# A long convolution and a cosine-gated layer on one core: the data as stationary operand of the last transform step, blocks of x turned by VectorE, and places of 129 elements

## The chip, the cores and the metric

The kernel runs on one core of a Trainium2 chip. The metric is device time in microseconds (us), from the start of the program to its end; lower is better. A core has a matrix engine (TensorE, PE in the profile; its weight loads are the row PEld), VectorE (DVE), ScalarE (ACT), GpSimd (POOL) and SyncE (SP), which here only issues DMAs. SP issues them in program order on one queue, and 16 DMA engines carry the packets.

## The reference

```python
# x, v (4, 12480, 128); pos_emb (12480, 64); w1 (64, 64); w2 (64, 128)
h = (np.maximum(pos_emb @ w1, 0) @ w2) * np.exp(-0.01 * pos)[:, None]
u = x * v
y = irfft(rfft(u, n=2*S, axis=1) * rfft(h, n=2*S, axis=0), n=2*S, axis=1)[:, :S]
t = (x * y).reshape(49920, 128)
hid = t @ w_in                        # 128 -> 2048
out = (hid * np.cos(hid)) @ w_out     # 2048 -> 128
```

All data are float32. The first part is a causal convolution along the sequence, channel by channel, with a filter h of the sequence's length; the second a layer with a cosine gate ("MoE" in the code's names).

## The kernel before, in words

**The convolution** is a transform of M = 96 x 120 points in two steps each way (N1 = 96, N2 = 120; the sequence is R = 104 rows of 120). One large array in SBUF, `slots`, holds a batch through all steps: per partition 64 pairs of channels, and for each pair 240 places of 2 elements (L807); `parts`, `above` and `aT` are views of it (L808 to L810). A *place* is the set of 128 channels that one index of the transform has in a partition; here its 64 pairs lie 480 elements apart. The steps of a batch:

- *u*: x and v are loaded (`load_pairs`, L373), multiplied (L395) and their sums and differences put into places (L401).
- *f1* (L405): for each of the 128 channels a matmul whose stationary operand ("weights") is the channel's column of `slots` and whose moving operand is a table of 192 columns; evicted (L420) to `parts`.
- *f2* (L442): for each of 48 pairs of indices k1, matmuls with a table `w` (124 partitions) as weights and 256 columns of `slots` moving, then the product with the filter's transform `h` on VectorE and GpSimd (L456). `w` and `h` come from the DRAM tensors `wd` and `hd`. For batch 0 a variant (`f2_both_units`, L610) makes `w` and `h`, uses them and stores them for the later batches.
- *i1* (L477): per channel two matmuls with the channel's column as weights and a table of 120 columns moving; evicted (L484) to places.
- *i2* (L493), the last step: 30 groups g of four indices n2. Each n2 takes two matmuls that add up: the weights are a table `t` (`tm`, 96 x 104), and the moving operand is a place, 128 channels. So a group's result is 104 rows by 4 x 128 channels in a PSUM bank. `i2_out` (L507) multiplies it by x, loaded in the same form as `xs` (L673), and stores it to the DRAM tensor `zd`, one row of 512 elements for each row and group (L517). The tables `tm` are made once in batch 0 (some ahead, L659) and loaded from `td` for the other batches.

While i2 of a batch runs, the loads, products and sums of the next batch run between its groups (`inverse_units`, L688).

**The layer** takes the rows of `zd` in 98 blocks n of up to 128 rows (the first has 104), that is up to 512 tokens of 128 channels, and 16 chunks c of 128 hidden units. `moe_load` (L723) fetches a block as rows (`zb`); `moe_turn` (L730) turns it to channels by tokens with four TensorE transposes (L126 in the profile, a helper's line) and a copy by ScalarE into `at`. A step (n, c) is: the up matmul (L743), ScalarE's scaled copy `a` (L746), VectorE's rounding `k` (L749), GpSimd's difference `f` (L752), ScalarE's sine `cs` (L757), VectorE's product `gt` (L759) and, four steps later (LAG), the down matmul into the accumulator `acc` (L768), which has one PSUM bank (once the convolution is through, every other block takes a bank of its pool). After the last chunk ScalarE copies `acc` to `ot` (L774), `moe_back` (L777) turns it back with four transposes and a copy `ob`, and `moe_store` (L786) stores it with one to three DMAs in runs of 1 KB.

**The order.** Instructions are issued in the order that the program writes them. Every step of the convolution is a generator (`units`, L530, whose parts are `before`: loads, `mm`: matmuls, `after`: evictions, each a `yield` apart). The generators say how many layer steps they are worth; the main loop (L949 to L974) issues one layer step, then as much of the convolution as is owed. So the layer runs beside the convolution of batches 1 to 3 and beside i2 of batch 0, and alone at the end. Until about 338 us the convolution runs alone: the filter, f1 of filter and batch 0, `f2_both` (171 to 270) and i1. `beside` (L876) puts conversions of the layer's weights between units of f1 and i1. i2 of the four batches stands at 338 to 565, 1178 to 1384, 1992 to 2206 and 2815 to 2946 us; the layer alone from about 3000.

All DMAs are issued by SP. Each kind of tile has a few buffers (`bufs`); an instruction that needs a buffer waits until its former user is done.

Of the kernel before, what the change touches and what calls it, by code (L numbers as in the profile page):

```python
# [9 lines left out]
F32 = mybir.dt.float32  # L10
# [20 lines left out]
def kernel(  # L31
# [74 lines left out]
    LAG = 4  # L106
    WCOL = 256

    dram = ctx.enter_context(tc.tile_pool(name="dram", bufs=1, space=DRAM))
    hd = dram.tile([N1 // 2, N2, 2, CB, 4], F32, name="hd")  # L110
    zd = dram.tile([NROWS, G, D], F32, name="zd")
# [241 lines left out]
    def filter_out(pool, bank, aT, slots, j, w2_sb):  # L353
# [5 lines left out]
        above = pool.tile([FR, 2, CB, 2], F32, name="above", bufs=2)  # L359
        pj = ps[0:FR, :].rearrange("p (n b i) -> p n b i", n=4, i=2)  # L360
        nc.scalar.copy(out=above[:, :, :, :], in_=pj[:, 2:4])
        a = H - 2 - 2 * j
        for place, op in ((a, ALU.add), (ODD + a, ALU.subtract)):
            nc.vector.tensor_tensor(
                slots[0:FR, :, place:place + 2, :].transpose([0, 2, 1, 3]),
                pj[:, 1::-1], above[:, :, :, :], op=op)
# [14 lines left out]
    def clear_gap(u):  # L381

        nc.gpsimd.memset(u[:, :, H:ODD, :], 0.0)
# [13 lines left out]
    def u_sums(u, tiles, a):  # L397
        both = tiles[0][:, :, :].rearrange("p h (n b i) -> p h n b i", n=UA, i=2)
        below, above = both[:, 0, ::-1, :, :], both[:, 1, :, :, :]
        for place, op, e in ((a, ALU.add, nc.gpsimd), (ODD + a, ALU.subtract, nc.vector)):  # L400
            e.tensor_tensor(u[0:R, :, place:place + UA, :].transpose([0, 2, 1, 3]),  # L401
                            below, above, op=op)


    def f1_mm(ps, u, b, i):  # L405

        nc.tensor.matmul(ps[0:KE, i * 2 * N1:(i + 1) * 2 * N1], u[:, b, 0:KE, i],  # L407
# [12 lines left out]
    def f1_evict(ps, b, share):  # L420
        copy, negated = f1_takers(b, share)
        pj = ps[:, 0:4 * N1].rearrange("p (i r k) -> p r k i", i=2, r=2)
        copy(out=parts[0:ODD, :, :, b, :], in_=pj[0:ODD])
        yield
        copy(out=parts[ODD:KE, 0, :, b, :], in_=pj[ODD:KE, 1])
        negated(parts[ODD:KE, 1, :, b, :], pj[ODD:KE, 0])
        yield

    def f1_evict_filter(ps, b, share):
# [3 lines left out]
        near, far = ftile[:, b, :, :], above[:, b, :, :]  # L433
# [8 lines left out]
    def f2_mm(ps, w, k1, i, filt=False):  # L442
# [3 lines left out]
        pi = ps[0:N2, :].rearrange("p (r b g i) -> p g r b i", r=2, g=2, i=2)[:, i]  # L446
        if not filt:
            nc.tensor.matmul(pi, w[:, i, :], parts[0:KE, :, k], start=True, stop=True)  # L448
        elif k < KF:
            both = ftile[0:KE, :, k:k + N1 + 1:N1, :].rearrange("p b r i -> p r b i")  # L450
            nc.tensor.matmul(pi, w[:, i, :], both, start=True, stop=True)
        else:
            for r, src in enumerate((ftile[0:KE, :, k, :], above[0:KE, :, k - KF, :])):
                nc.tensor.matmul(pi[:, r], w[:, i, :], src, start=True, stop=True)

    def f2_product(pool, ps, h, k1, whole):  # L456


        y = parts[0:N2, :, k1:k1 + 2, :, :].rearrange("p r k b i -> p r b (k i)")
        t = pool.tile([N2, 2, CB, 4], F32, name="t", bufs=1 + whole)  # L460
        uu = ps[0:N2, :].rearrange("p (r b j) -> p r b j", r=2, j=4)
# [15 lines left out]
    def i1_mm(ps, b, i):  # L477
        for r in range(2):
            nc.tensor.matmul(  # L479
                ps[0:N1, (i * 2 + r) * N2:(i * 2 + r + 1) * N2],  # L480
                parts[0:N2, r, :, b, i],
                cs[:, r, :], start=True, stop=True)

    def i1_evict(pool, ps, b):  # L484
# [3 lines left out]
        for h, op in ((0, ALU.add), (1, ALU.subtract)):  # L488
            nc.vector.tensor_tensor(slots[0:N1, b, h * N2:(h + 1) * N2, :], pj[:, 0],  # L489
                                    other[:, :, :], op=op)  # L490
            yield

    def i2_mm(ps, t, g, part):  # L493
        for i in range(part * G // 2, (part + 1) * G // 2):
# [8 lines left out]
            for r, place in enumerate(places):  # L503
                nc.tensor.matmul(ps[0:R, i * D:(i + 1) * D], t[:, i, r, :],  # L504
                                 slots[0:N1, :, place, :], start=(r == 0), stop=(r == 1))

    def i2_out(pool, ps, xs, b, g):  # L507
        if b == 0:
            yield
        zs = pool.tile([R, 2, UA, D], F32, name="zs")  # L510
        nc.vector.tensor_tensor(
            zs[:, :, :, :].rearrange("p h n d -> p (h n d)"), ps[0:R, :],
            xs[:, :, :].rearrange("p h n -> p (h n)"), op=ALU.mult)
        z = zs[:, :, :, :].rearrange("p h n d -> p (h n) d")
        row = (b * NG + g) * R
        if row > 0:
            nc.sync.dma_start(zd[row:row + R, :, :], z)  # L517
        else:
            zbs[0] = z
        made[0] += 1  # L520
        yield

# [482 lines left out]
```

## Time and profile before

| | before |
|---|---|
| device time, median of 3 runs | 3760.59 us (3759.83 to 3761.09) |
| profiled execution, span | 3758.9 us |
| up matmul L743: records, busy, mean | 3136, 1599.0 us, 591 ns |
| ScalarE copies L737, L774, L783, mean | 574, 574, 584 ns |
| place matmul L504: records, busy, mean | 1920, 251.7 us, 273 ns |
| f2's matmul L448: records, busy, mean | 576, 173.0 us, 380 ns |
| GpSimd's sums L474: records, mean | 384, 821 ns |

The profile is of one execution. A matmul of 512 columns leaves two records, one of 256 columns or fewer leaves one. Matmuls are pipelined, so records overlap and a mean duration is longer than the pace; the pace is read from start to start. "x" behind an engine's time is the count of instructions in a stretch; a wait is written as the waiting instruction, "<-", and what released it, then the total idle time in us, the count and the mean. PEclk is the granted clock of TensorE; it is 1.00 or near it over nearly the whole span.

### The profile page before, as it was taken

Reading aid. Unit: us, or ns where it says so; the run is one execution under the profiler, and the core shown is the slowest. Engines: PE = TensorE matmul, PEld = TensorE weight load, DVE = VectorE, ACT = ScalarE, POOL = GpSimd, SP = SyncE. Lnnn points to the kernel's source line nnn. Section 1 sums busy time; section 2 is a strip of 40 time slices with the busy share of each in tenths; the row PEclk is TensorE's granted clock in tenths of the full one; section 3 lists DMA queues with packets and bytes.
Section 4 is the critical chain, followed back from the end, with each engine's and each line's share of the span. In section 5 each row is a group of like instructions: output and inputs, shape, how many; then the busy total and the mean of one; then the engine's idle time right before and its main releaser. Section 6 shows DMA issues by size and latency. Waiting matters only on the chain.

```text
span 3758.9 us, 47177 instructions
## 1 busy us (share of the span) xinstructions
PE 3690.6 (98%) x13546; PEld 2110.4 (56%) x13546; DVE 2773.7 (74%) x5586; ACT 2508.2 (67%) x4660; POOL 2557.6 (68%) x2318
## 2 busy tenths in 40 slices
PE   7898999999999999999999999999999999999999
PEld 6777555555566556555565556555566544444444
DVE  8887997687866787788766776788765666666666
ACT  5757776766665557766665567666664677777777
POOL 6666776588845665688745664788644677777776
PEclk9999999999999999999999999999999999999999
DMA  6263551022203650122104530122105200000000
GB/s 167 64 185 107 155 167 33 25 72 79 72 12 91 181 151 12 40 79 77 52 18 128 180 105 21 52 79 76 38 21 172 76 23 17 17 23 18 17 23 13
DMA packets 209499, 276.14 MB, mean 73 GB/s; under 512 B 17111, under 2 KB 146535, under 8 KB 209111
## 3 DMA queue, kind: packets, MB, share of 16 engines
q1 hardware_dynamic: 209239, 273.12, 24.8%
q8 instruction: 109, 1.79, 0.2%
q14 instruction: 151, 1.24, 0.1%
HBM read 193.64 MB, written 79.42 MB: 73 GB/s over the span
## 4 chain that ended last, share of the span: by engine, by line
PE 88%; DVE 3%; POOL 3%; ACT 2%; DMA 2%; issue 1%; SPq 0%; POOLq 0%; DVEq 0%; ACTq 0%
PE ph L743 33%; PE acc L768 28%; PE cv L504 5%; PE cv L768 5%; PE cv L479 4%; PE cv L407 3%; PE cv L448 3%; PE ph L126 2%; POOL f L752 1%; PE ps L407 1%; PE ps L448 1%; DMA tm<-td 1%; DMA wd<-w 1%; ACT cs L757 1%; DVE k L749 1%
## 5 line engine op out<-in xcount | busy, mean ns | idle before, releaser
L752 POOL TENSOR_TENSOR f<-a,k 128x512 f32<-128x512 f32 (+1 forms) x1568 | 1986.2, 1267 | 1060.5 <-DVE k L749 1059.1
L743 PE MATMUL ph<-at,w_in_sb 128*128 128x512 f32 (+1 forms) x3136 | 1599.0, 591 | 3.7 <-DVE gt L759 2.7
L746 ACT ACTIVATE a<-ph,quarter 128x512 f32<-128x512 f32 (+1 forms) x1568 | 1071.2, 683 | 704.8 <-PE ph L743 695.2
L768 PE MATMUL acc<-gt,w_out_sb 128*128 128x512 f32 (+1 forms) x2688 | 1370.3, 591 | 0.0
L759 DVE TENSOR_TENSOR gt<-ph,cs 128x512 f32<-128x512 f32 (+1 forms) x1568 | 1077.3, 687 | 359.9 <-ACT cs L757 341.8
L757 ACT ACTIVATE cs<-f 128x512 f32<-128x512 f32 (+1 forms) x1568 | 981.0, 626 | 366.6 <-POOL f L752 364.3
L749 DVE TENSOR_SCALAR k<-a 128x512 f32<-128x512 f32 (+1 forms) x1568 | 792.9, 506 | 550.7 <-ACT a L746 524.2
L768 PEld LDWEIGHTS acc<-gt,w_out_sb 128*128 128x128 f32 x2688 | 508.4, 189 | 642.8 <-issue 631.9
L743 PEld LDWEIGHTS ph<-at,w_in_sb 128*128 128x128 f32 x3136 | 553.2, 190 | 337.7 <-issue 257.5
L474 POOL TENSOR_TENSOR slots<-slots,t 120x256 f32<-120x256 f32 x384 | 312.9, 821 | 59.9 <-DVE t L467 25.6
L504 PEld LDWEIGHTS cv<-slots,tm 96*104 96x104 f32 x1920 | 238.6, 169 | 106.8 <-issue 85.4
L504 PE MATMUL cv<-slots,tm 96*104 96x128 f32 x1920 | 251.7, 273 | 9.9 <-POOL tm L297 5.0
L768 PE MATMUL cv<-gt,w_out_sb 128*128 128x512 f32 (+1 forms) x448 | 224.5, 583 | 1.0 <-DVE gt L759 1.0
L479 PEld LDWEIGHTS cv<-cs,slots 120*96 120x96 f32 x1536 | 176.7, 167 | 67.2 <-issue 65.2
L479 PE MATMUL cv<-cs,slots 120*96 120x120 f32 x1536 | 183.2, 266 | 0.0
L448 PEld LDWEIGHTS cv<-slots,w 124*120 124x120 f32 x576 | 103.7, 184 | 124.3 <-issue 112.3
L407 PEld LDWEIGHTS cv<-c,slots 104*124 104x124 f32 x768 | 132.6, 192 | 72.2 <-issue 60.0
L448 PE MATMUL cv<-slots,w 124*120 124x256 f32 x576 | 173.0, 380 | 0.0
L407 PE MATMUL cv<-c,slots 104*124 104x192 f32 x768 | 151.8, 327 | 5.4 <-DVE gt L759 3.5
L768 PEld LDWEIGHTS cv<-gt,w_out_sb 128*128 128x128 f32 x448 | 84.9, 190 | 104.8 <-issue 99.5
L489 DVE TENSOR_TENSOR slots<-cv,other 96x240 f32<-96x240 f32 x384 | 133.1, 394 | 1.5 <-ACT other L487 1.4
L395 DVE TENSOR_TENSOR xt<-xt,vt 104x256 f32<-104x256 f32 x177 | 132.6, 751 | 0.6 <-DMA vt<-in_v_dram 0.6
(131 smaller groups left out, 2520.9 us busy)
## 6 DMA issues: line engine op xcount, KB each, us to landing
h<-hd SPq DMA_DIRECT2D x144, 240.0 KB
tm<-td SPq DMA_DIRECT2D x96, 312.0 KB
xt<-in_x_dram SPq DMA_DIRECT2D x120, 208.0 KB
vt<-in_v_dram SPq DMA_DIRECT2D x120, 208.0 KB
xs<-in_x_dram SPq DMA_DIRECT2D x120, 208.0 KB
zd<-zs SPq DMA_DIRECT2D x119, 208.0 KB
zb<-zd SPq DMA_DIRECT2D x96, 256.0 KB
w<-wd SPq DMA_DIRECT2D x144, 116.2 KB
```

The source lines that it names most:

```text
L407: nc.tensor.matmul(ps[0:KE, i * 2 * N1:(i + 1) * 2 * N1], u[:, b, 0:KE, i], c1[0:u.shape[0], :, :].rearrange("p r k -> p (r k)"), start=Tr ...
L448: nc.tensor.matmul(pi, w[:, i, :], parts[0:KE, :, k], start=True, stop=True)
L474: nc.gpsimd.tensor_tensor(y[:, r], y[:, r], t[:, r], op=op)
L479: nc.tensor.matmul(ps[0:N1, (i * 2 + r) * N2:(i * 2 + r + 1) * N2], parts[0:N2, r, :, b, i], cs[:, r, :], start=True, stop=True)
L504: nc.tensor.matmul(ps[0:R, i * D:(i + 1) * D], t[:, i, r, :], slots[0:N1, :, place, :], start=(r == 0), stop=(r == 1))
L743: nc.tensor.matmul(ph[:, 0:m], w_in_sb[:, c * P:(c + 1) * P], ats[n][:, 0:m], start=True, stop=True)
L746: nc.scalar.activation(a[:, 0:m], ph[:, 0:m], AF.Identity, bias=quarter[:, 0:1], scale=INV_TWO_PI)
L749: nc.vector.tensor_scalar(out=k[:, 0:m], in0=a[:, 0:m], scalar1=ROUND, scalar2=ROUND, op0=ALU.add, op1=ALU.subtract)
L752: nc.gpsimd.tensor_tensor(f[:, 0:m], a[:, 0:m], k[:, 0:m], op=ALU.subtract)
L757: nc.scalar.activation(cs[:, 0:m], f[:, 0:m], AF.Sin, scale=TWO_PI)
L759: nc.vector.tensor_tensor(gt[:, 0:m], ph[:, 0:m], cs[:, 0:m], op=ALU.mult)
L768: nc.tensor.matmul(accs[n][:, 0:m], w_out_sb[:, c, :], gt[:, 0:m], start=(c == 0), stop=(c == NFC - 1))
```

## The change

1. *Places of 129 elements.* `slots` becomes [partitions, 240 places, 129 elements], the 128 channels of a place side by side and one element unused. The filter's transform in the first stage (`ftile`) is laid out in the same way. A channel's column (the weights of f1 and i1) is thereby read with a step of 516 bytes in place of 8; a place (the moving operand of f2) is contiguous. Evictions of f1 and i1 write pairs of channels, 516 bytes from one pair to the next.
2. *The last step.* In i2 the place becomes the weights (96 x 128 channels) and the table the moving operand (104 columns). The result is 128 channels by 4 x 104 rows, which is the form in which the layer takes it.
3. *x by blocks.* x has to have the same form. `blocks_units` copies x from DRAM to a DRAM tensor `xd`, 64 DMAs per batch in runs of 32 elements; these are issued between units of f1 of the batch (of f1 and `f2_both` for batch 0). `blocks_load` fetches a group's blocks with four DMAs of 32 partitions (`xb`, three buffers), a group ahead; VectorE turns each with a transpose by squares of 32 (`xt`, one instruction of 128 x 416), issued behind the group before.
4. *The layer's input.* `zd` is stored as channels by rows, and `moe_load` fetches `at` directly, in one to three DMAs, half a block ahead. `zb`, `moe_turn` and its transposes and copy go. Batch 0's first group is written straight to `at`.
5. *The layer's output.* VectorE takes `acc` out of PSUM with a transpose by squares of 32 in place of ScalarE's copy; `moe_back` goes. `moe_store` becomes a generator: for each piece of a block that belongs to one group, 16 DMAs of 8 partitions in runs of 32 elements, four issued per layer step from c = 6 on. In the last block half of them are issued by ScalarE.
6. *Small moves.* `above` of `filter_out` lies in unused places; the table `cs` is loaded behind `f2_both` in place of ahead of it; the identity for transposes is gone after the filter.

```diff
-    hd = dram.tile([N1 // 2, N2, 2, CB, 4], F32, name="hd")
-    zd = dram.tile([NROWS, G, D], F32, name="zd")
+    SQ = 32
+    DP = D + 1
+    ROWB = SQ // G
+    NB = R // ROWB
+    hd = dram.tile([N1 // 2, N2, 2, 2, D], F32, name="hd")
+    xd = dram.tile([B, H, D // SQ, UA, ROWB, NB, SQ], F32, name="xd")
+    zd = dram.tile([B * NG, D, G, R], F32, name="zd")
...
-        nc.tensor.matmul(ps[0:KE, i * 2 * N1:(i + 1) * 2 * N1], u[:, b, 0:KE, i],
+        nc.tensor.matmul(ps[0:KE, i * 2 * N1:(i + 1) * 2 * N1], u[:, 0:KE, 2 * b + i],
...
-                nc.tensor.matmul(ps[0:R, i * D:(i + 1) * D], t[:, i, r, :],
-                                 slots[0:N1, :, place, :], start=(r == 0), stop=(r == 1))
+                nc.tensor.matmul(ps[0:D, i * R:(i + 1) * R], slots[0:N1, place, 0:D],
+                                 t[:, i, r, :], start=(r == 0), stop=(r == 1))
...
+    def blocks_units(b):
+        for a in range(D // SQ):
+            for i in range(UA):
+                for r in range(ROWB):
+                    start = x[b, r * N2 + i, a * SQ:(a + 1) * SQ]
+                    nc.sync.dma_start(
+                        xd[b, :, a, i, r, :, :],
+                        bass.AP(tensor=start.tensor, offset=start.offset,
+                                ap=[[UA * D, H], [ROWB * N2 * D, NB], [1, SQ]]))
+                    yield
+    def blocks_load(t, b, g):
+        first, _, second, _ = n2s(g)
+        for a in range(D // SQ):
+            start = xd[b, first // UA, a, 0, 0, 0, :]
+            nc.sync.dma_start(
+                t[a * SQ:(a + 1) * SQ, :, :],
+                bass.AP(tensor=start.tensor, offset=start.offset,
+                        ap=[[(second - first) // UA * (D // SQ) * UA * ROWB * NB * SQ, 2],
+                            [NB * SQ, UA * ROWB], [1, NB * SQ]]))
+    def blocks_turn(pool, t):
+        xt = pool.tile([D, G, R], F32, name="xt", bufs=2)
+        nc.vector.transpose(xt[:, :, :].rearrange("d i (n r) -> d n i r", r=ROWB),
+                            t[:, :, :].rearrange("p n (i r) -> p n i r", r=ROWB))
+        return xt
...
     def moe_load(pool, n):
-        zb = pool.tile([P, G, D], F32, name="zb", bufs=2)
-        nc.sync.dma_start(zb[0:m, :, :], zd[row:row + m, :, :])
+        at = pool.tile([D, BANK], F32, name="at")
+        to = at[:, 0:G * m].rearrange("d (i n) -> d i n", i=G)
+        done = 0
+        while done < m:
+            group, n1 = divmod(row + done, R)
+            rows = min(m - done, R - n1)
+            nc.sync.dma_start(to[:, :, done:done + rows], zd[group, :, :, n1:n1 + rows])
+            done += rows
...
-        ot = pool.tile([D, BANK], F32, name="ot", bufs=1)
-        nc.scalar.copy(out=ot[:, 0:m], in_=accs.pop(n)[:, 0:m])
+        ot = pool.tile([P, BANK // SQ, SQ], F32, name="ot", bufs=2)
+        nc.vector.transpose(
+            ot[:, 0:m // ROWB, :],
+            accs.pop(n)[:, 0:G * m].rearrange("d (i n r) -> d n i r", i=G, r=ROWB))
...
+            for i, n2 in enumerate(n2s(g)):
+                for a in range(D // SQ):
+                    start = out[b * S + n1 * N2 + n2, a * SQ:(a + 1) * SQ]
+                    first = a * SQ + i * ROWB
+                    issuers[a % 2].dma_start(
+                        bass.AP(tensor=start.tensor, offset=start.offset,
+                                ap=[[N2 * D, ROWB], [ROWB * N2 * D, count // ROWB],
+                                    [1, SQ]]),
+                        ot[first:first + ROWB, at:at + count // ROWB, :])
+                    yield
...
-            slots = spool.tile([P, CB, 2 * N2, 2], F32, name="slots")
+            slots = spool.tile([P, 2 * N2, DP], F32, name="slots")
...
-                if n == 0 and c == NFC // 2:
-                    load(1)
-                if c == NFC - 4 and n + 2 < NALL:
-                    load(n + 2)
+                if c == NFC // 2 and n + 1 < NALL:
+                    load(n + 1)
...
-                if c == (LAG - 1 if n else NFC - 2) and n + 1 < NALL:
-                    moe_turn(mpool, n + 1)
-                if c == NFC // 2 and n - 1 in ots:
-                    obs[n - 1] = moe_back(mpool, n - 1, ots.pop(n - 1))
-                if c == NFC // 2 + 2 and n - 1 in obs:
-                    moe_store(n - 1, obs.pop(n - 1))
+                if c == LAG + 2 and n - 1 in ots:
+                    for _ in stores:
+                        pass
+                    stores = moe_store(n - 1, ots.pop(n - 1))
+                if c != LAG - 1:
+                    for _ in range(4):
+                        next(stores, None)
```

## The prediction, made before the changed kernel had run

> **What bounds the kernel now.** I read the page first (span, part 1, the DMA lines), then TensorE's timeline, which tells pace from waiting, then the table by stage, whose bounds are the first and last matmul of a stage.
>
> ```profile
> span 3758.9 us, 47177 instructions
> PE 3690.6 (98%) x13546; PEld 2110.4 (56%) x13546; DVE 2773.7 (74%) x5586; ACT 2508.2 (67%) x4660; POOL 2557.6 (68%) x2318
> ...
> DMA packets 209499, 276.14 MB, mean 73 GB/s; under 512 B 17111, under 2 KB 146535, under 8 KB 209111
> ...
> q1 hardware_dynamic: 209239, 273.12, 24.8%
> ```
>
> TensorE is busy 98%, DMA 24.8%. That a busy TensorE is also at its pace, the timeline shows:
>
> ```profile
> 1203.26 1.05 PE L504 MATMUL cv<-slots,tm 96*104 96x128 f32 x8
> 1204.15 1.02 PE L743 MATMUL ph<-at,w_in_sb 128*128 128x512 f32 x2
> 1205.01 1.02 PE L768 MATMUL acc<-gt,w_out_sb 128*128 128x512 f32 x2
> ...
> 1210.20 0.60 PE L126 MATMUL ph<-ident,ot 128*128 128x128 f32 x4
> 1210.63 1.05 PE L504 MATMUL cv<-slots,tm 96*104 96x128 f32 x8
> ```
>
> Start to start, a 512-column matmul (two records) takes 0.86 us, eight 128-column records of L504 0.89 (111 ns each), four transposes 0.43 (107 ns each), with nothing between. So columns removed from TensorE are time saved, where nothing else is close behind. The stages in which something is:
>
> ```profile
> core 0: us, PE busy (x) PEld busy (x) DVE busy (x) ACT busy (x) POOL busy (x), PEclk, DMA share, GB/s
> 171.40:270.00 98.60, 95.86 (x480) 74.51 (x480) 83.97 (x189) 53.36 (x142) 64.79 (x92) 0.98 0.59 172
> 338.00:565.00 227.00, 223.88 (x914) 131.97 (x915) 205.65 (x362) 165.78 (x330) 171.37 (x161) 0.99 0.54 164
> 1177.60:1383.50 205.90, 204.25 (x861) 120.28 (x860) 157.27 (x279) 113.58 (x187) 130.70 (x112) 1.00 0.59 176
> 1992.20:2206.40 214.20, 211.36 (x877) 123.07 (x876) 161.03 (x287) 119.03 (x195) 135.68 (x116) 1.00 0.57 171
> 2814.70:2945.70 131.00, 131.00 (x676) 87.61 (x675) 67.41 (x119) 58.03 (x98) 56.92 (x45) 1.00 0.57 168
> ```
>
> The first row is the second step with the filter (f2_both), the others the last step (i2) of the four batches. In all five DMA is busy 54 to 59% as a mean of 16 engines, and in f2_both that mean already binds. Its waits:
>
> ```profile
> ACT h L630 <- DMA hd<-h: 35.1, 38, 1.4
> ```
>
> Why at 59%? The packet records give typical times (medians): 4 bytes 9 ns, 256 18, 512 34, 960 44, 1024 46, 1664 69, 2048 84, 3328 131. They also show how many engines a DMA uses: each engine closes its share with a 4-byte packet. If a DMA runs on the largest number up to 16 that divides its outermost count (104 rows: 13; 124 rows: 4; 120: 15), the 1341 DMAs need 16,983 such packets; the trace has 16,984. So `wd<-w` (124 rows) loads four engines with 31 packets, `hd<-h` (120) fifteen with 8. If the same low engines serve every DMA, one of them moves 48 x (31 x 44 + 8 x 84) ns = 98 us: the stage's 98.6. A few engines are the limit there, not the mean.
>
> **The change, part by part.**
>
> *TensorE.* 784 transposes (L126, eight for each of 98 blocks) go: 784 x 107 ns = 84 us. Of these about 148 lie in the i2 stages and 636 (68 us) outside. The i2 matmul moves 104 columns in place of 128: 1920 records x 24/128 x 111 ns = 40 us, all in i2. MoE, f1, f2 and i1 keep their columns.
>
> *ACT, VectorE, GpSimd.* ACT loses three copies a block (574, 584, 574 ns: 170 us), and was no bound. VectorE gains 98 turns of 128x512 out of PSUM (as L759, 690 ns: 68 us) and 120 turns of 128x416 (between L749's 471 and L759's 586: 60 us), and loses 11 us at L511 (680 to 586 ns). In the tightest stage, 338 to 565, that is 205.7 + 16 of 227: below what DMA will need. The turn now frees the one `acc` bank and stands behind `k` (507 ns) in VectorE's queue: 0 to 0.25 us a block, 0 to 18 us; I take 5.
>
> *Places of 129.* Weights of f1 and i1 are read one element in 516 bytes, before one in 8; no row shows that. From below 0: L479's record (8-byte step, 96 columns, 167 ns) is no longer than L504's contiguous one (104 columns, 169). From above: a load wholly exposed makes an i1 record last 167 ns in place of 102 and an f1 record 192 in place of 164: 2048 x 65 + 1280 x 28 ns = 169 us. I take 0, the nearer row. Evictions now write pairs 516 bytes apart: between nothing and double L489's 394 ns, which would put i1 at 2.5 us a unit on VectorE against 2.25 now, some 55 us; I take 0, since VectorE has that room otherwise. The f2 sums on GpSimd become contiguous; it waits anyway.
>
> The Trainium skill speaks against it: SBUF — State Buffer, section "Door 1: The DMA port swizzle (why `[64,N]` ≈ `[32,N]`)", notes that accesses need two hits in each 16-byte line to run at full rate. By it the 169 us would be nearer than 0; no run here has shown it.
>
> *DMA.* The built program issues 5203 DMAs (1341 before), 654,864 data packets (192,256). New: x by blocks to DRAM (256 DMAs of 780 packets of 128 bytes, 60 rows: 15 engines); blocks loaded (480 DMAs of 32 packets of 1664 bytes, outermost count 2 in DRAM, 32 in SBUF); stores (3344 of 8 rows: 8 engines, 128-byte packets); `at` from `zd` (106,496 packets of at most 416 bytes). On SP an issue takes 0.30 to 0.40 us (`out<-ob` 0.30 to 0.40, `xs` 0.31): 5200 x 0.35 = 1820 us, and four stores beside a 1.71 us step are 1.3 us: free, unless delayed. A 128-byte packet costs 13 ns by the line through the sizes, 46 if small ones cost as 1 KB; I take 18 (256 bytes).
>
> The blocks decide. By the divisor rule 2 and 32 share 2: two engines with 16 packets a DMA, four DMAs a group: 64 x 69 ns = 4.4 us a group. All rows of before have equal counts on both sides, so the bounds are 2 and 16 engines (4.4 and 0.55 us); I take 2, as `wd<-w` shows that an uneven count is not spread.
> The Trainium skill has a rule for unequal counts: DMA: Bandwidth & Descriptors, section "Why a DMA increments its semaphore by 16 and not by 1", has the number of engines divide the slowest dims of both sides, and take the lowest-numbered ones. By it the group costs the 4.4 us; by sixteen engines 0.55. For equal counts the trace agrees (16,983 of 16,984).
>
> Load of the busiest engine in i2, per group: blocks 4.42; x and v of the next batch 32 x 46 = 1.47 (not in the last); `tm` or `td` 6 x 131 = 0.79; `zd` 8 x 69 = 0.55. Per MoE block of 16 steps: stores 256 x 18 = 4.6, `at` 64 x 18 = 1.2. Thirty groups, with 97, 85, 89 and 44 MoE steps counted in the stages, 3 to 4 us of 9 ns packets, less the blocks fetched before the stage starts (9 us; 13 in the last), give 247, 242, 244 and 179 us. TensorE would need 207, 187, 194 and 117 there. Against 227, 206, 214 and 131 now: +20, +36, +30, +48 = **+134**. VectorE waits for blocks in order, so MoE and TensorE wait with it.
>
> In f2_both, already on its engines, half of batch 0's blocks are written: 32 x 52 packets x 18 ns = **+30**. In later f1 stages 3328 x 18 = 60 us per engine fit into 131.
>
> Sum: -68 + 134 + 30 + 5 = +101 on 3758.9, so 3860 for the execution; the median stands 1.7 above its span: **3862**.
>
> **Rivals.**
> - *DMA stays hidden: faster.* If the blocks are split by their 32 SBUF rows, or each DMA takes other engines, i2 is TensorE's again. In the second batch TensorE needs 6.2 us a group and the other loads 3.9, which leaves room for 33 packets: it decides from four engines on. Then -84 - 40 + 5: 3641. For it: mean DMA 25%. Against: f2_both. 13%.
> - *About even.* Fewer us lost (packets without queueing, more prefetch) and the sums cancel within 0.2%, about what a measurement of this kernel tells from no change: 3%.
> - *Strided weights exposed.* +169 beside the forecast: 4031. The i1 and f1 stages decide. 5%.
> - *Small packets dear.* At 46 ns instead of 18: i2 +141, f2_both +46, and f1 becomes DMA's (153 + 37 against 131, +59 three times): +364, 4226; in between at 30 ns some 4000. 9%.
> - Forecast, with its own 3790 to 3960: 70%.
>
> **How the numbers follow.** Faster 13%. Slower is the forecast, both dear cases: 84%. Same 3%. The range leaves out the hidden case and the upper half of the dear ones, and reaches down to no change, which packets without any queueing and unhurried f2_both would give: 3755 to 4050.
>
> **What would show it.** Right: in the four i2 windows PE busy falls well under 95%, the wait of VectorE's turn of x for the DMA of the blocks leads the waits, windows last near 180 to 250 us; f2_both near 130; each block load closes with two 4-byte packets; the late stage (3000 on) runs 27.3 us a block instead of 28.2. Wrong: sixteen closing packets, i2 windows shorter than before, or longer i1 and f1 windows with PE's records stretched (strides), or SP's own issue time filling the MoE stage.

## The result, and the profile after

The changed kernel takes 4169.74 us (median of 4 runs, 4165.71 to 4179.59) against 3760.84 (median of 4); the ratio is 1.109 (95% interval 1.1077 to 1.1108). The direction was forecast, the size was not: +409 us in place of +101, outside the range of 3755 to 4050. The profiled execution has a span of 4164.5 us.

The page of the changed kernel, the lines that answer to those of before:

```profile
span 4164.5 us, 49552 instructions
PE 3897.7 (94%) x12762; PEld 2298.7 (55%) x12762; DVE 2839.0 (68%) x5804; ACT 2415.6 (58%) x4366; POOL 2527.7 (61%) x2316
...
DMA packets 701439, 301.97 MB, mean 73 GB/s; under 512 B 552275, under 2 KB 664035, under 8 KB 701027
...
q1 hardware_dynamic: 700387, 298.71, 29.4%
```

TensorE is busy for 207 us more, though it executes 784 records fewer: some records have become slower. The rest of the 406 us is idle time. The table by stage (f2_both, then the four i2 stages, each from its first to its last matmul) shows where:

```profile
core 0: us, PE busy (x) PEld busy (x) DVE busy (x) ACT busy (x) POOL busy (x), PEclk, DMA share, GB/s
183.20:298.40 115.20, 95.52 (x480) 74.27 (x480) 82.99 (x188) 52.74 (x139) 59.59 (x91) 0.99 0.70 173
397.00:661.00 264.00, 233.73 (x868) 134.86 (x868) 206.94 (x395) 159.12 (x314) 170.78 (x160) 0.93 0.46 134
1309.90:1596.40 286.50, 230.71 (x832) 130.54 (x831) 170.66 (x321) 110.11 (x178) 129.92 (x116) 0.91 0.44 125
2248.00:2536.40 288.40, 232.41 (x833) 130.10 (x831) 171.34 (x321) 110.08 (x178) 129.98 (x116) 0.91 0.43 124
3182.40:3371.80 189.40, 152.48 (x656) 94.14 (x655) 78.92 (x151) 55.21 (x90) 56.15 (x46) 0.90 0.37 114
```

In i2 TensorE is 80 to 89% busy, and the DMA share has fallen from 54–59% to 37–46%: something holds up the transfers, and it is not their mean load. Measured in the same way, all stages together give the account of the 405.6 us:

| stages | before | after | difference |
|---|---|---|---|
| i2, four batches | 778.1 | 1028.3 | +250.2 |
| i1, four batches | 489.7 | 604.5 | +114.8 |
| f1, filter and four batches | 499.8 | 543.7 | +43.9 |
| f2_both | 97.9 | 115.2 | +17.3 |
| f2, three batches | 859.5 | 849.5 | -10.0 |
| behind the last i2 | 813.2 | 792.7 | -20.5 |
| between the stages | | | +9.9 |

i2 and i1 make nine tenths of it. The windows of i1 and f1 before also hold 156 transposes, 17 us, that are gone after, so i1 and f1 have lost 175 us to something else. i1 was forecast to lose only its transposes. TensorE's timeline in i1 of the second batch, first of the kernel before:

```profile
1044.96 0.98 PE L479 MATMUL cv<-cs,slots 120*96 120x120 f32 x8
1045.78 1.03 PE L743 MATMUL ph<-at,w_in_sb 128*128 128x512 f32 x2
```

and of the changed kernel:

```profile
1141.86 1.48 PE L484 MATMUL cv<-cs,slots 120*96 120x120 f32 x8
1143.17 1.03 PE L797 MATMUL ph<-at,w_in_sb 128*128 128x512 f32 x2
```

Start to start, eight records take 0.82 us before and 1.31 after, 102 and 164 ns each, with no idle time in either. Counts and shapes are the same; what the change did to these matmuls is the step of the weights. In i2 the same view shows idle time (in brackets, with what ended it), and slow records behind it:

```profile
1424.31 1.11 PE L509 MATMUL cv<-tm,slots 96*128 96x104 f32 x8 [1.55 <-DMA tm<-td]
1425.25 1.78 PE L797 MATMUL ph<-at,w_in_sb 128*128 128x512 f32 x2
1426.83 1.91 PE L822 MATMUL acc<-gt,w_out_sb 128*128 128x512 f32 x2
1428.54 1.18 PE L509 MATMUL cv<-tm,slots 96*128 96x104 f32 x8
...
1433.01 1.04 PE L509 MATMUL cv<-tm,slots 96*128 96x104 f32 x8
1433.88 1.04 PE L797 MATMUL ph<-at,w_in_sb 128*128 128x512 f32 x2
```

TensorE's longest wait in this whole window (1310 to 1596):

```profile
PE cv L509 <- DMA tm<-td: 55.4, 20, 6.3
```

Three things are to be seen. TensorE waits for the tables `tm`, whose DMA is as it was, and not for the blocks of x. After a wait a pair of 512-column records takes 1.58 to 1.71 us (1425.25 to 1426.83, and on to 1428.54) in place of 0.86: the clock records show 0.50 from 1425.4 us on, for 3.4 us. Such stretches make the 0.91 of the table. And undisturbed, eight records of L509 take 0.87 us (1433.01 to 1433.88), 109 ns each, though they move 104 columns where they moved 128 in 111 ns.

### The profile page after: what moved, and what is told of

It is laid out like the page before. It is cut to its first block, busy times and chain, and to the rows that moved or that the text cites. A ratio compares the mean times of both kernels' runs of the same rounds, so it can differ in the third digit from the quotient of the medians.

```text
span 4164.5 us, 49552 instructions
## 1 busy us (share of the span) xinstructions
PE 3897.7 (94%) x12762; PEld 2298.7 (55%) x12762; DVE 2839.0 (68%) x5804; ACT 2415.6 (58%) x4366; POOL 2527.7 (61%) x2316
## 4 chain that ended last, share of the span: by engine, by line
PE 70%; DMA 14%; DVE 5%; POOL 4%; SPq 3%; issue 2%; ACT 2%; DVEq 0%; POOLq 0%; ACTq 0%
PE ph L797 25%; PE acc L822 21%; PE cv L484 6%; PE cv L822 4%; PE cv L411 4%; DMA vt<-in_v_dram 4%; DMA tm<-td 3%; POOL f L806 3%; PE ps L411 3%; PE cv L509 2%; DMA hd<-h 2%; PE ps L484 2%; PE cv L453 2%; DMA xb<-xd 2%; DVE k L803 1%
## 5 line engine op out<-in xcount | busy, mean ns | idle before, releaser
L797 PE MATMUL ph<-at,w_in_sb 128*128 128x512 f32 (+1 forms) x3136 | 1635.5, 603 | 20.6 <-DVE gt L813 13.3
L822 PE MATMUL acc<-gt,w_out_sb 128*128 128x512 f32 (+1 forms) x2688 | 1397.8, 602 | 21.9 <-DVE ot L828 21.7
L803 DVE TENSOR_SCALAR k<-a 128x512 f32<-128x512 f32 (+1 forms) x1568 | 755.3, 482 | 769.7 <-ACT a L800 745.2
L509 PEld LDWEIGHTS cv<-tm,slots 96*128 96x128 f32 x1920 | 269.3, 209 | 295.9 <-issue 194.6
L509 PE MATMUL cv<-tm,slots 96*128 96x104 f32 x1920 | 277.2, 293 | 155.4 <-DMA tm<-td 145.6
L479 POOL TENSOR_TENSOR slots<-slots,t 120x256 f32<-120x256 f32 x384 | 290.5, 762 | 84.6 <-DVE t L472 48.8
L484 PEld LDWEIGHTS cv<-cs,slots 120*96 120x96 f32 x1536 | 290.8, 266 | 64.2 <-issue 63.7
L484 PE MATMUL cv<-cs,slots 120*96 120x120 f32 x1536 | 281.4, 330 | 0.0
L411 PEld LDWEIGHTS cv<-c,slots 104*124 104x124 f32 x768 | 195.9, 312 | 60.3 <-issue 33.2
L411 PE MATMUL cv<-c,slots 104*124 104x192 f32 x768 | 188.3, 375 | 1.9 <-DVE gt L813 1.9
L549 DVE TENSOR_TENSOR zs<-cv,xt 128x416 f32<-128x416 f32 x119 | 69.2, 581 | 100.0 <-DMA zd<-zs 92.7
```

Of the source, the lines that this page charges most:

```text
L479: nc.gpsimd.tensor_tensor(y[:, r], y[:, r], t[:, r], op=op)
L484: nc.tensor.matmul(ps[0:N1, (i * 2 + r) * N2:(i * 2 + r + 1) * N2], parts[0:N2, r, :, 2 * b + i], cs[:, r, :], start=True, stop=True)
L509: nc.tensor.matmul(ps[0:D, i * R:(i + 1) * R], slots[0:N1, place, 0:D], t[:, i, r, :], start=(r == 0), stop=(r == 1))
L797: nc.tensor.matmul(ph[:, 0:m], w_in_sb[:, c * P:(c + 1) * P], ats[n][:, 0:m], start=True, stop=True)
L803: nc.vector.tensor_scalar(out=k[:, 0:m], in0=a[:, 0:m], scalar1=ROUND, scalar2=ROUND, op0=ALU.add, op1=ALU.subtract)
L822: nc.tensor.matmul(accs[n][:, 0:m], w_out_sb[:, c, :], gt[:, 0:m], start=(c == 0), stop=(c == NFC - 1))
```

## Experiments

Theory after the result: (A) strided weights double the time of a weight load, which costs i1 and f1; (B) in i2 the blocks' loads fill two engines; (C) i2's matmul is bound by its 128 weight columns. Rivals: the evictions in 516-byte steps for A, SP's time for B, moving columns for C.

**The pace of matmuls by themselves (p1_pace).** TensorE alone, nothing of the reference computed.

```diff
+for j in range(32):
+    nc.tensor.matmul(ps[0:cols, 0:m], big[0:k, j % 4:j % 4 + (cols - 1) * stride + 1:stride],
+                     mov[0:k, 0:(m - 1) * ms + 1:ms], start=True, stop=True)
```

> TensorE alone: groups of 32 matmuls, weights of a given number of columns (w), step between them in elements (s; 1 where not named) and moving columns (m); t is a step of the moving operand. It computes nothing of the reference. Theory: the pace start to start is 0.85 ns times the larger of moving columns and weight columns, where weight columns count double once their step leaves less than two of them in 16 bytes: w128m104 109 ns, w104m128 109, w96m120 102, w128m32 109, w64m104 89; s2 102, s4 and above 164, the same for 128, 129 and 240. Rival for the last step: the pace follows moving columns alone: w128m104 89 ns, w128m32 near 30. Rival for the steps: banks, powers of two (64, 128) slower than 129, and 129 near full pace.

Its timeline, one line a group of 64 records:

```profile
69.09 13.92 PE L46 MATMUL w128m64x<-mov,big 96*128 96x64 f32 x64 [0.28 <-DVE res L48]
83.29 13.98 PE L46 MATMUL w128m104x<-mov,big 96*128 96x104 f32 x64 [0.28 <-DVE res L48]
...
126.03 5.95 PE L46 MATMUL w96m104x<-mov,big 96*96 96x104 f32 x64 [0.28 <-DVE res L48]
...
152.67 6.81 PE L46 MATMUL s2w96m120x<-mov,big 120*96 120x120 f32 x64 [0.27 <-DVE res L48]
...
168.78 11.56 PE L46 MATMUL s4w96m120x<-mov,big 120*96 120x120 f32 x64 [0.28 <-DVE res L48]
...
237.43 11.40 PE L46 MATMUL s129w96m120x<-mov,big 120*96 120x120 f32 x64 [0.28 <-DVE res L48]
```

Start to start, in ns a record: 96 weight columns with 104 moving 89, with 120 moving 102; 104 with 128 moving 109; 64 with 64 moving 58. 128 weight columns stand in a stretch at half the clock (0.50): 213 for 64 and 104 moving alike, that is some 107 at full clock. So in these groups the larger of the two counts sets the pace, at 0.85 to 0.91 ns a column, and i2's swap (104 weights and 128 moving to 128 and 104) could gain nothing: C holds, as the 109 ns of L509 at full clock say too. Steps of the weights, 96 columns and 120 moving: step 2 102, step 3 132, step 4 177, 5 167, 8 180, 16 165, 64 and 128 167, 129 174, 130 185, 240 164. The loss is complete from 16 bytes on, and powers of two are no worse: A's rule holds, with a factor of 1.6 to 1.8, and the rival of banks falls. With 512 moving columns a step of 129 is hidden (429, the pace of 512 columns).

**The strided weights in the kernel (e3_near_weights).** Beside e1_sixteen, which follows.

```diff
-u[:, 0:KE, 2 * b + i],
+near[0][0:u.shape[0], at:at + KE] if made[0] else u[:, 0:KE, 2 * b + i],
...
-parts[0:N2, r, :, 2 * b + i],
+near[0][0:N2, (2 * b + i) * 8:(2 * b + i) * 8 + N1],
```

> As e1_sixteen, and the weights of i1 (all batches) and of f1 (batches 1 to 3) are read from neighbouring elements of another table in place of the channels' columns: this leaves out the channels' data in these two steps, and keeps the same counts and shapes. Theory, strided weights: a record of i1 goes from 164 to 102 ns and of f1 from 212 to 164, so 2048 x 62 + 768 x 48 = 164 us less than e1_sixteen, about 3740; i1 windows near 140 in place of 172. Rival: the evictions, which write pairs 516 bytes apart, bind these steps: i1 windows stay above 160.

One run, 3915.83 us; span 3914.1 against 4074.3 of e1_sixteen: 160.2 us less. The windows of i1 are 60.8 and three times 138.8 us in place of 89.5 and three times 171.6. Since the evictions still write in steps of 516 bytes, these cost nothing that shows. The groups of i1's weight loads, e1_sixteen and then e3_near_weights (busy, mean ns of one):

```profile
L484 PEld LDWEIGHTS cv<-cs,slots 120*96 120x96 f32 x1536 | 290.8, 266 | 64.2 <-issue 63.7 <-POOL f L807 0.5
```

```profile
L488 PEld LDWEIGHTS cv<-cs,w_in_sb 120*96 120x96 f32 x1536 | 176.2, 163 | 77.3 <-issue 77.3
```

The expectation was 164 us less. A is shown, to within 4 us of its price.

**Sixteen engines for the blocks (e1_sixteen).**

```diff
-            start = xd[b, first // UA, a, 0, 0, 0, :]
-            nc.sync.dma_start(t[a * SQ:(a + 1) * SQ, :, :], ... ap=[[..., 2], [NB * SQ, UA * ROWB], [1, NB * SQ]])
+            for half, n2 in enumerate((first, second)):
+                start = xd[b, n2 // UA, a, 0, 0, 0, :]
+                at = a * SQ + half * UA * ROWB
+                nc.sync.dma_start(t[at:at + UA * ROWB, :, :], ... ap=[[NB * SQ, UA * ROWB], [1, NB * SQ]])
```

> The changed kernel, but each group's blocks of x are fetched by eight DMAs of 16 rows (one for each half of 32) in place of four of 2 x 16 rows: same bytes, same packets. Theory, engines: four DMAs of outermost count 2 put 64 packets of 1664 bytes on two engines, and these bind the last step; with 16 on both sides the closing 4-byte packets rise from 46,291 to 60,691 and the i2 windows fall to what TensorE needs, that is the windows of before less their transposes: about 222, 206, 207 and 129 us in place of 264, 287, 288 and 189, so about 3905 in all. There the place matmul keeps its pace of 109 ns a record (no gain from 104 columns). Rival, SP: it is the issuing on SP that binds (30 groups of 2.4 us of block loads beside the stores); eight issues of 0.3 us take as long, so the time stays at 4165. Rival, bytes: the mean load of all engines binds; then also no change.

4076.45 us, ratio 1.0840 (1.0824 to 1.0856): 93 us less than the changed kernel, a third of what B promised. The i2 windows are 254.8, 256.6, 260.5 and 167.0. So the two engines were a limit, and right behind them stands another. SP's timeline points to it; one group of the second i2:

```profile
1416.11 0.34 SPq L723 DMA_DIRECT2D tm<-td  x1
1416.50 5.26 SPq L531 DMA_DIRECT2D xb<-xd  x8
1421.86 0.37 SPq L556 DMA_DIRECT2D zd<-zs  x1
1422.33 0.35 SPq L381 DMA_DIRECT2D xt<-in_x_dram  x1
1422.77 0.40 SPq L381 DMA_DIRECT2D vt<-in_v_dram  x1
```

SP goes from issue to issue and has 7.1 us of them before the next group's table can be asked for, or more where stores follow; in the whole window 196 of 256 us are issues (blocks 89, stores 56). TensorE would need 6.9 us a group. The rival of SP was wrong in its number (no change was expected); whether SP is the next limit the runs below ask.

**Stores issued by ScalarE in i2 (e4_stores_by_act).**

```diff
-issuers[a % 2].dma_start(
+by_act = last_step[0] or last and a % 2
+(nc.scalar if by_act else nc.sync).dma_start(
```

> As e1_sixteen, but while the last step of a batch runs, the layer's stores are issued by ScalarE in place of SP (700 of 3344). Same DMAs, same bytes. In e1_sixteen SP issues for 196 us of the 256 us of the second i2 window (176 stores 56 us, blocks 89 us), and waits in order for most of the rest. Theory, SP's queue: with 56 us of issues gone from it the tables (tm) are asked for earlier, TensorE's 32 us of idle time and the clock of 0.93 that goes with it shrink, and the i2 windows fall from 255, 257, 261 and 167 to 215 to 235 and about 145: some 3980 in all. Rival, engines or DMA: the stores' packets hold up the tables; the same packets then give the same windows and 4075. Rival, ScalarE: its 1.3 us a step of issues delays the layer; windows longer than in e1_sixteen.

4105.72 us, ratio 1.0919 (1.0905 to 1.0934): slower than e1_sixteen, as the rival of ScalarE had it. The first three windows grew to 268.8, 259.6 and 267.8 us. TensorE's waits in the second i2, first of e1_sixteen:

```profile
PE cv L509 <- DMA tm<-td: 31.9, 13, 4.3
```

and here, where they are no longer for the tables alone:

```profile
PE ph L802 <- DVE gt L818: 15.4, 7, 4.4
PE acc L827 <- DVE ot L833: 12.1, 5, 4.2
PE cv L509 <- DMA tm<-td: 10.1, 7, 2.6
```

The wait for `tm` has gone from 31.9 to 10.1 us, but the issues now stand in ScalarE's order between the activations that the layer waits for. In this window ScalarE's 180 issues take 55 us, and it waits another 58 us ahead of them for earlier DMAs to land; ScalarE's own longest wait is

```profile
ACT a L805 <- DMA out_dram<-ot: 60.8, 24, 6.5
```

Why a store waits for an earlier DMA stands in the last section. So this is more than the 1.3 us a step that the rival reckoned with. In the last i2, with half of the layer steps, the window did shrink (167.0 to 161.3). This run alone settles nothing about SP.

**Two issues a group in place of eight (e8_two_loads).**

```diff
+        for half, n2 in enumerate(n2s(g)[::UA]):
+            nc.sync.dma_start(t[half::2, :, :],
+                              xd[b, n2 // UA].rearrange("a i r n e -> (a i r) n e"))
...
-            xt[:, :, :].rearrange("d i (n r) -> d n i r", r=ROWB),
-            t[:, :, :].rearrange("p n (i r) -> p n i r", r=ROWB))
+            xt[:, :, :].rearrange("d (h i) (n r) -> d n i r h", h=2, r=ROWB),
+            t[:, :, :].rearrange("p n (i r h) -> p n i r h", r=ROWB, h=2))
```

> The changed kernel with a group's blocks fetched by two DMAs of 64 rows (one for each half; the squares' rows are ordered with the half innermost, and VectorE's turn sorts them out): sixteen engines as in e1_sixteen, and two issues in place of eight. Theory, SP's issuing: per group SP has 8 x 0.46 + 1.7 us and some 2.3 us of stores in e1_sixteen, 7.7 us where TensorE needs 6.9; with two issues it has about 4.9, so the i2 windows fall from 255, 257, 261 and 167 to TensorE's 222, 206, 207 and 129, perhaps 10 us more each for waits, and the whole to 3905 to 3945. Rival: SP is not it (e4_stores_by_act took 56 us of issues from SP and got slower): the windows stay as in e1_sixteen, 4076.

3968.99 us, ratio 1.0556 (1.0538 to 1.0574), another 107 us less; the windows are 241.9, 230.8, 226.9 and 131.9. Three are 20 to 25 us longer than TensorE was said to need, the last 3 us. The second, in the table by stage:

```profile
1288.10:1518.90 230.80, 213.30 (x832) 121.52 (x831) 173.28 (x320) 110.16 (x178) 130.07 (x115) 0.98 0.56 154
```

The blocks of a group in SP's timeline, eight issues of 5.26 us above, are now:

```profile
1381.04 1.09 SPq L527 DMA_DIRECT2D xb<-xd  x2
```

The DMA share is back at 0.54 to 0.58 in the four windows, nearly that of before, and the clock at 0.98 in this one. SP's issues have fallen from 196 to 135 us in the second window, with the same bytes and again sixteen engines: the number of issues on SP was the second limit. The time is 24 us above the range expected.

**The output side alone on the kernel before (e2_output_side), and its stores taken apart.** VectorE's turn of `acc` and the 128-byte stores, put into the kernel before; nothing else of the change.

```diff
-nc.scalar.copy(out=ot[:, 0:m], in_=accs.pop(n)[:, 0:m])
+nc.vector.transpose(ot[:, 0:m // ROWB, :],
+                    accs.pop(n)[:, 0:G * m].rearrange("d (i n r) -> d n i r", i=G, r=ROWB))
```

> The kernel before, with the output side of the change alone: VectorE turns acc out of PSUM by squares of 32, stores in runs of 128 bytes, four DMAs a step; four of the eight transposes of a block and two copies by ScalarE go. Theory: 392 transposes of 107 ns = 42 us less, the stores are free (13 ns a packet), the turn in VectorE's queue costs up to 0.3 us a block at acc: 3720 to 3745. Rival: the stores or VectorE's turn hold up the layer, 3760 or above.

3786.13 us, ratio 1.0069 (1.0052 to 1.0086): 0.7% slower, though 392 transposes are gone. The second and third i2 windows are 224.0 and 231.4 us (205.8 and 214.3 before), and the program ends 15.7 us after the last down matmul began, in place of 5.6. Two further kernels ask what does it in i2.

e10_no_stores_i2:

```diff
+if last_step[0]:
+    continue
 issuers[a % 2].dma_start(
```

> As e2_output_side, with the stores that fall into the last step of a batch left out (764 of 3344; those rows of the result are not written). e2_output_side's second and third i2 windows are 224 and 231 us in place of 206 and 214. Theory: the stores do it, by SP's time (184 x 0.32 us = 59 us in the second window) and their packets; without them the windows are 203 and 210 or below. Rival: VectorE's turn of acc does it; the windows stay at 224 and 231.

e11_thin_stores:

```diff
+kept = 1 if last_step[0] else count // ROWB
...
-ap=[[N2 * D, ROWB], [ROWB * N2 * D, count // ROWB], [1, SQ]]
+ap=[[N2 * D, ROWB], [ROWB * N2 * D, kept], [1, SQ]]
```

> As e2_output_side, but a store that falls into the last step of a batch moves one row of runs only, 8 packets in place of up to 104 (the other rows are not written); the number of issues on SP stays. Windows of i2, second and third batch: 224 and 231 us in e2_output_side, 202 and 209 without these stores. Theory, SP's time: issues of 0.3 us stay, so the windows stay above 218 and 225. Rival, packets: 128-byte packets on the eight low engines hold up the tables; then 202 to 208 and 209 to 215.

One run each: 3743.53 and 3785.05 us. The second i2 in the table by stage, e2_output_side, then e10_no_stores_i2, then e11_thin_stores:

```profile
1174.00:1397.50 223.50, 206.09 (x837) 117.20 (x836) 161.59 (x284) 108.52 (x176) 130.51 (x112) 0.99 0.58 161
```

```profile
1176.00:1378.20 202.20, 202.16 (x841) 118.31 (x840) 160.35 (x285) 109.04 (x177) 131.07 (x112) 1.00 0.57 173
```

```profile
1175.00:1399.90 224.90, 208.06 (x841) 118.95 (x840) 161.44 (x284) 108.66 (x177) 130.66 (x113) 0.98 0.53 155
```

Without the stores TensorE is at its pace; with the stores' issues but hardly any of their packets the loss is whole here, and 20.0 of 22.8 us in the third window. So it is neither the 128-byte packets nor VectorE's turn, but the stores' number on SP. Their issues take 56 us of this window (0.305 us each), and SP waits another 14 us for earlier DMAs to land, which it does nowhere in e10_no_stores_i2. SP is not full in sum (107 of 225 us are issues), but the next group's loads stand behind the stores in its order:

```profile
1251.45 4.06 SPq L796 DMA_DIRECT2D out_dram<-ot  x12
1255.61 0.33 SPq L378 DMA_DIRECT2D xs<-in_x_dram  x1
1256.04 0.34 SPq L679 DMA_DIRECT2D tm<-td  x1
```

Issues and waits were not separated.

**The copies of x out of f2_both (e5_xd_in_f1).**

```diff
-                        if i % 4 == 0:
+                        if i % 2 == 0:
                             next(blocks, None)
...
-            for i, _ in enumerate(f2_both_units(bank)):
-                if i % 6 == 0:
-                    next(blocks, None)
+            for _ in f2_both_units(bank):
+                pass
```

> As e1_sixteen, but all 64 copies of batch 0's x to blocks are issued between units of f1 and none between those of f2_both. Theory: f2_both (116 us) falls to the 98 us of before, since 32 x 52 packets of 13 ns = 22 us on each of fifteen engines leave it, and f1 of batch 0 (117 us, bound by TensorE with strided weights) takes them up. Rival: f2_both has another reason (places of 129 in its products and evictions) and stays at 115.

One run, 4064.93 us, 12 less than e1_sixteen. f2_both:

```profile
190.10:288.40 98.30, 95.30 (x479) 74.37 (x480) 83.21 (x188) 52.24 (x137) 59.60 (x91) 0.98 0.59 171
```

98.3 us, as before the change (97.9): the whole loss there comes from the copies. Their issues on SP left together with their packets (31 of 0.86 us each); since SP's issues fill only 57 of the 115 us in the changed kernel, while the DMA share is 0.70, the packets are the likelier part, but that was not separated.

**All three mended (e9_all_mended).** e8_two_loads with the edits of e3_near_weights and e5_xd_in_f1.

> As e8_two_loads, with the weights of i1 and f1 read from neighbouring elements as in e3_near_weights (the channels' data left out) and batch 0's copies as in e5_xd_in_f1. If the three causes add up: e8_two_loads less 160 and less 12, some 3735 to 3770; then little is left of the change's loss, and what it gains (68 us of transposes) is partly lost to the last store (12 us) and f1 of the filter and batch 0 (15 us). Rival: the causes overlap, 3850 or more.

One run, 3805.26 us; span 3803.4 against 3967.5 of e8_two_loads. The two edits bring 164 of the 172 us expected; the total is 35 us above the range, which had been worked out from a lower time for e8_two_loads. Even so mended, with the channels' data left out of i1 and f1, it is some 44 us slower than the kernel before: i2 still has 831 us against 778.

**A version that beats both (e6_input_side), and one that doesn't (e7_both_sides_act).** Only the layer's input is turned by VectorE, with four loads a block and without a change to places, i2, x or stores.

```diff
+        for a in range(D // SQ):
+            start = zd[row, 0, a * SQ:(a + 1) * SQ]
+            nc.sync.dma_start(zb[a * SQ:(a + 1) * SQ, 0:m // ROWB, :],
+                bass.AP(tensor=start.tensor, offset=start.offset,
+                        ap=[[D, SQ], [ROWB * G * D, m // ROWB], [1, SQ]]))
...
+            nc.vector.transpose(at[:, 0:G * m].rearrange("d (n f) -> d n f", f=SQ),
+                                zb[:, 0:m // ROWB, :])
```

> The kernel before, with the turn of the layer's input by VectorE: the rows of zd are fetched in squares (four DMAs of 32 partitions and 128-byte runs in place of one), VectorE turns them by squares of 32, four of the eight TensorE transposes of a block and one copy by ScalarE go; the stores stay as before, in runs of 1 KB. Theory: 388 transposes of 107 ns less, about 42 us, with three more issues of SP for a block: 3715 to 3730. Rival: what made e2_output_side slower is VectorE's turn or the 128-byte runs as such, and not the 16 stores a piece on SP; then 3760 or above.

3747.45 us, ratio 0.9966 (0.9954 to 0.9978): 12 us (0.3%) faster than the kernel before, and faster than the changed one by 422; but 30 us short of the 42 expected. In the layer alone a block of 512 tokens takes 28.01 us in place of 28.34, so 0.33 us of the 0.43 that four transposes are; in the f2 stages nothing is gained (286.5, 288.8 and 286.2 against 286.4, 286.7 and 286.4), where VectorE is now busy 242 of 286 us. Where the gain went there was not tried.

> The kernel before with both turns by VectorE (input as in e6_input_side, output as in e2_output_side), and every second store issued by ScalarE. Theory: all transposes of the layer go (84 us), and SP has half of the stores; if SP's issuing is what cost e2_output_side its gain, 3680 to 3720. Rival: ScalarE, with 2 issues of 0.3 us in a step, takes the gain away: 3740 and above.

Both turns, and every second store issued by ScalarE: 3776.03 us, ratio 1.0039 (1.0025 to 1.0053). The layer alone gets its 0.88 us a block (28.34 to 27.47), 22 us behind the last i2; but the first three i2 windows lose 8, 13 and 12 us, and f2 another 8. By e11_thin_stores the stores' issues are the likely cause in i2; it was not taken apart here.

## Why the prediction was wrong

The forecast was 305 us short. Strided weights, put at 0, make 175 of it, and i2, put at +134 and measured at +250, makes 116; the other terms together make 14.

- **Strided weights: the failed step, first part.** The prediction took 0, because L479's weight load with its step of 8 bytes was no longer than L504's contiguous one, with 169 us as the upper end. The runs show 160 us for i1 and f1 of batches 1 to 3 (e3_near_weights), and the f1 stage of filter and batch 0, which e3 leaves strided, is 15 longer, with weight loads busy for all of its 117 us (89 of 102 before). The row was true but did not bear on 516 bytes: a step of 8 bytes still has two elements in 16 bytes, 516 bytes has one. The note of the Trainium skill in SBUF — State Buffer, section "Door 1: The DMA port swizzle (why `[64,N]` ≈ `[32,N]`)", which the prediction set aside, asks for two hits in each 16-byte line, and p1_pace agrees: 102 ns at a step of two elements, 132 at three, 177 at four. The rival of 4031 (5%) had this mechanism.
- **SP: the failed step, second part.** "four stores beside a 1.71 us step are 1.3 us: free, unless delayed" weighed SP against the layer alone. In i2 SP also issues the blocks, `tm`, `zd`, x and v; there, in the second batch, its issues come to 174 us in the changed kernel and 196 in e1_sixteen, in windows that TensorE needs 206 for, and in the changed kernel SP waits another 63 us there for earlier DMAs to land (last section). e8_two_loads (107 us) and e11_thin_stores show the cost.
- **The two engines.** Right in kind: the closing packets are 46,291, which is the number for the built program if a DMA of unequal counts runs on a common divisor, two for 2 and 32. The Trainium skill, DMA: Bandwidth & Descriptors, section "Why a DMA increments its semaphore by 16 and not by 1", states that rule; the count agrees, e1_sixteen has 14,400 more (960 DMAs of sixteen in place of 480 of two), and it gains 93 us. Mis-sized: the terms used median packets (69, 46, 131 ns); the means in the second i2 are 78, 58 and 184. By an estimate from these a group costs 64 x 78 + 32 x 58 + 6 x 184 + 8 x 78 ns = 8.6 us, and thirty with the layer's 20 us of stores (5.5 blocks x 256 packets x 14 ns) 277, against 242 forecast and 286 measured. The forecast of the waits was wrong too: TensorE waits for `tm`, and not VectorE for the blocks. The tables themselves land a median 3.0 us after their issue (3.7 before; times from their semaphores); they are asked for late, because SP waits for earlier DMAs to land, block loads above all (median 5.2 us to landing, 2.4 in e1_sixteen).
- **The last step's 24 columns** (40 us, used for what TensorE needs in i2) were never to be had: weights of 128 columns set 109 ns. That made the rival of 3641 too good: sixteen engines, its condition, gave 4076.
- **Small packets** were put at 18 ns; they take 13, and f2_both lost 17 us in place of 30, to the copies as named (e5_xd_in_f1). Dear small packets (9%) fell.
- **Transposes.** As forecast behind the last i2: 27.47 us a block in place of 28.34. In f2 the three stages gave 10 us in place of 22. Left out of the sum was the last block's store: the program ends 18.0 us after the last down matmul began, in place of 5.6.
- **Evictions in 516-byte steps at 0**: right, by the windows of e3_near_weights.

Of i2's 250 us, 89 go with the two engines and 107 with the blocks' issues on SP, in this order of the edits (e1_sixteen itself adds 25 us of block issues to the second window). Most of the last 53 would be the stores on SP, if they cost beside these windows what they cost beside those of e2_output_side (45 us); that was not tried on the changed kernel.

## What to carry to other kernels

Ask of every operand that becomes strided whether two elements still lie in 16 bytes, for weights as for moving data, and count a matmul by the larger of weight columns and moving columns (here up to 192; with 512 moving columns the stride was hidden). Count a queue's issues in the stage where they fall and beside everything else that it issues there: a store that is free beside one loop takes the place of a load beside another. Look also at which semaphores the DMAs take: if they are few, a slow DMA holds up later ones that need nothing of it. And a DMA whose outermost counts differ (here 2 and 32) runs on a common divisor of them: making them equal brought 93 us here, and making the DMAs fewer 107, more than the 68 us of transposes that the change was to save outside i2.

## What the runs showed that was not expected

The clock goes with the stalls: the i2 windows of the changed kernel ran at 0.90 to 0.93 (33 of its 40 stretches of half clock lie there), those of e8_two_loads at 0.96 to 1.00, so that a wait can cost again after it is over, as in the timeline above. The moving operand behaves like the weights in p1_pace: 256 moving columns take 226 ns with a step of two elements, 453 with four and 460 with eight.

And SP was held up where nothing that it needs is named. In the second i2 of the changed kernel:

```profile
SPq L843 <- DMA xb<-xd: 31.1, 37, 1.5
SPq L529 <- DMA xb<-xd: 14.2, 17, 1.4
```

These stores (L843) and block loads (L529) use nothing of the block load that they wait for. The trace's semaphores (counters by which a DMA tells that it has landed) give the reason: the DMAs of SP, and of ScalarE where it issues any, take eight semaphores in turn, and each of these waits is for the DMA eight issues earlier, which has the same semaphore, to land. So no more than eight are on their way, and a slow DMA holds up SP eight issues later. In the second i2 such waits take 63 us in the changed kernel, 18 in e1_sixteen, 14 in e8_two_loads, 13 in e2_output_side, 14 in e11_thin_stores, and nothing in the kernel before or in e10_no_stores_i2. In e4_stores_by_act, where two engines share the eight, they take 66 us on SP and 58 on ScalarE. This is how block loads on two engines reach the tables, and a second cost of many small DMAs beside their issue time. What more semaphores would bring was not tried.
